# Another sequence for the same operations: a WKV recurrence and a mixer MLP on one core

## The chip, the core and the metric

The kernel runs on one NeuronCore of one Trainium2 chip. The metric is the device time of one execution in microseconds; the time before is the median of three runs, 478.63 us (478.45 to 481.3). Five engines work in parallel, each through its own queue in order: TensorE (PE, with its weight loads as PEld), VectorE (DVE), ScalarE (ACT), GpSimd (POOL) and SyncE (SP), which here only starts transfers. They wait for each other through semaphores.

## The reference

```python
def _attn_ref(r, k, v, w, u):            # (B,H,S,D) = (4, 8, 768, 48)
    for t in range(S):
        cur = einsum('bhd,bhe->bhde', u[None] * kt, vt)
        y[:, :, t] = einsum('bhd,bhde->bhe', rt, state + cur)
        state = wt[:, :, :, None] * state + einsum('bhd,bhe->bhde', kt, vt)

def _moe_ref(x, w_tok1, w_tok2, w_ch1, w_ch2):   # x: (4, 768, 384); d_tok 256, d_ch 1536
    h = maximum(xt @ w_tok1, 0) @ w_tok2         # xt: x with tokens and channels swapped
    u = x + h.transpose(0, 2, 1)
    return u + maximum(u @ w_ch1, 0) @ w_ch2
```

The output of the first function, its heads put side by side, is the `x` of the second.

## The kernel before

**Units.** A batch's 768 tokens fall into three units of 256, so four batches give twelve units, numbered 0 to 11. The recurrence runs in chunks of 64 tokens, four to a unit. Within a unit, for all eight heads at once:

- `load_part` and `load_w`, `load_v` bring k, r (tiles `rk`, for unit 2 a part of the tile `first`), the decays w and the values v. SP starts all of these.
- DVE scans the decays backwards (`ends`, L431 to L436) and forwards (`begins`, L443) and multiplies keys (L440) and queries (L446) by them.
- ACT multiplies keys by u (`own_u`, L331, tile `near`); PE makes the chunk's own products (`own_gram`) and the products with earlier tokens (`gram`), both at L315; DVE takes them into the tile `at` (`own_put` L458, `mask` L327).
- PE turns the keys (`tokens`, L345), ACT copies them out (`copied`, L350), PE makes the chunks' outer products in the PSUM tile `kv` (`carry`, L365).
- The state passes from chunk to chunk: ACT scales it into the tile `before` (`scaled`, L501, four instructions, called by0 to by3 below, one for each chunk) and PE adds it into `kv` by a product with the identity (`update`, L508, called up0 to up3; from unit 3 on DVE adds, L516). by1 needs up0, up1 needs by1, and so on into the next unit.
- PE multiplies queries with states (`across`, L380, called `before` in the sequence), ACT reads one column (`seen`, L389 or L392), PE adds the products within the chunks (`within`, L401, called `after`) and ACT puts the sum into `x` (`taken`, L407).
- ACT checks the decays' range (`ranges`, called small and large, L427).

**Weights** arrive as 64-bit words and are made into float32 in pieces of 1024 columns, three for the token mixer (t0 to t2) and nine for the channel mixer (c0 to c8). Each piece is a load (L261), two steps on ACT (plus L264, minus L267) and four on DVE (lead L270, two L273, value L277, sum L281).

**Mixers.** For batch 0, `hidden` (L947, called h0 to h11), its ReLU (`rectified`, L950), `back` (L958, with the sum into x at L960), `turn` (L969, copied to `xT` at L971), `up` (L993, ReLU L996) and `down` (L1004) run on float32 weights. For batches 1 to 3 `exact_mixing` runs the same in three float32r passes each (L667, L726, L741, L772 to L792), with weight parts that ACT, DVE and POOL split off ("forms", L579 to L601), some of which go to DRAM and come back through a ring of ten slots (L626).

**What sets the sequence.** Nothing is left to a scheduler. `strict(...)` ties each instruction to the one before it on its engine, in the order of its arguments. Before batch 0's second mixing half, these arguments are a list written out in the code (three units, three token pieces, the first channel piece). After that `interleaved(ORDER, ...)` merges ten streams of pieces; each digit of the string `ORDER` says which stream gives the next piece. `behind(gate, f)` adds a wait to a transfer: it isn't started before `gate` has run.

The first channel product (`up` at L993) is the point from which PE works through batch 0's channel mixer and everything that follows.

## Time and profile before

| | |
|---|---|
| three runs | 478.63 us median, 478.45 to 481.3 |
| the profiled execution, its own time | 478.31 us |
| its span, first to last instruction | 476.5 us |
| busy time on DVE, ACT, POOL | 344.6, 265.8, 54.2 us |
| bytes moved | 85.34 MB, mean 179 GB/s |

The span is what the trace shows; 1.8 us of the execution lie around it. A row of the timeline has the start in us from the span's start, the length in us, engine, line, operation, output and inputs, the count of instructions that follow each other, and in brackets the idle time of the engine before the row and what ended it. A PE row's length includes the drain of its last product, so that the start of the next row is the better end. A row of waits has engine, its line, what it waited for, us in total, how often, and the longest. A float32 product shows as two matmul records, so that the twelve h steps are 24 records.

### The profile page before, as it was taken

What the parts mean: (1) busy time and instruction counts of PE and PEld (TensorE: products, weight loads), DVE (VectorE), ACT (ScalarE), POOL (GpSimd) and SP (SyncE); (2) the same over time, 40 slices, a digit from 0 to 9 for tenths busy, and PEclk for the clock granted to TensorE, in tenths of its full rate; (3) what the DMA queues carried; (4) which work ended last, traced back from release to release, by engine and by line L of the source; (5) the groups of instructions that cost most, each with busy time, mean ns of one, the idle gap of its engine ahead of it and who ended that gap; (6) DMA issues with size and microseconds to landing.
All of it is one profiled execution on the core that took longest, in us unless ns stands there. A gap on an engine that the chain in (4) does not pass through costs nothing.

```text
span 476.5 us, 12778 instructions
## 1 busy us (share of the span) xinstructions
PE 459.1 (96%) x5322; PEld 409.6 (86%) x5322; DVE 344.6 (72%) x495; ACT 265.8 (56%) x606; POOL 54.2 (11%) x58
## 2 busy tenths in 40 slices
PE   3899999999999999999999999999999999999996
PEld 2776588856797668999999999999999999999995
DVE  7998797679598877876897998685587885235341
ACT  6699876674678856453747385351837554134140
POOL 1000000000000001231302002130304003032130
PEclk9999999999999999999999999999999999999999
DMA  8865745573584556963888842754784513336331
GB/s 313 317 221 217 188 169 191 180 275 99 152 228 138 177 179 207 284 186 100 252 283 232 294 154 56 198 173 141 215 227 150 167 61 84 115 101 199 86 99 54
DMA packets 45055, 85.34 MB, mean 179 GB/s; under 512 B 4736, under 2 KB 37376, under 8 KB 44992
## 3 DMA queue, kind: packets, MB, share of 16 engines
q1 hardware_dynamic: 44704, 84.37, 56.3%
q8 instruction: 43, 0.70, 0.6%
q14 instruction: 20, 0.16, 0.1%
q10 hardware_dynamic: 288, 0.10, 0.1%
HBM read 72.65 MB, written 11.80 MB: 177 GB/s over the span
## 4 chain that ended last, share of the span: by engine, by line
PE 90%; ACT 4%; DVE 2%; DMA 2%; issue 1%; SPq 0%; DVEq 0%; ACTq 0%
PE bank L1004 10%; PE bank L772 8%; PE bank L779 8%; PE bank L774 8%; PE bank L790 8%; PE bank L792 8%; PE bank L791 8%; PE bank L993 7%; PE bank L667 3%; PE bank L989 3%; PE bank L726 3%; PE bank L315 2%; PE bank L401 2%; PE bank L380 2%; PE kv_ps L365 2%; PE bank L669 2%
## 5 line engine op out<-in xcount | busy, mean ns | idle before, releaser
L765 POOL TENSOR_TENSOR z_high<-z_high 128x384 fp32r<-128x384 f32 x48 | 52.9, 1107 | 406.7 <-DMA ring<-third 186.8
L754 ACT ACTIVATE z_high<-bank 128x384 fp32r<-128x384 f32 x48 | 23.5, 489 | 58.1 <-PE bank L779 57.7
L772 PE MATMUL bank<-x_forms,forms 128*128 128x384 f32 x216 | 50.3, 341 | 0.0
L779 PE MATMUL bank<-z_more,forms 128*128 128x384 f32 x216 | 50.1, 340 | 0.0
L774 PE MATMUL bank<-x_forms,ring 128*128 128x384 f32 x216 | 49.3, 337 | 0.0
L761 DVE SCALAR_TENSOR_TENSOR z_high<-bank,z_high 128x384 fp32r<-128x384 f32 x48 | 26.5, 554 | 31.4 <-ACT z_high L754 29.4
L1004 PE MATMUL bank<-wch,z 128*128 128x384 f32 x144 | 48.1, 488 | 0.0
L790 PE MATMUL bank<-forms,z_high 128*128 128x384 f32 x140 | 47.8, 342 | 0.0
L792 PE MATMUL bank<-forms,z_high 128*128 128x384 f32 x140 | 47.1, 337 | 0.0
L791 PE MATMUL bank<-ring,z_high 128*128 128x384 f32 x140 | 47.1, 337 | 0.0
L798 DVE SCALAR_TENSOR_TENSOR x<-bank,x 128x384 f32<-128x384 f32 x35 | 18.8, 553 | 39.0 <-PE bank L792 38.9
L1004 PEld LDWEIGHTS bank<-wch,z 128*128 128x128 f32 x144 | 26.8, 190 | 17.2
L501 ACT ACTIVATE before<-state,to_end 112x48 f32<-112x48 f32 x132 | 33.1, 324 | 13.0 <-DVE state L516 7.6
L779 PEld LDWEIGHTS bank<-z_more,forms 128*128 128x128 f32 x216 | 39.0, 188 | 0.1
L772 PEld LDWEIGHTS bank<-x_forms,forms 128*128 128x128 f32 x216 | 38.3, 188 | 0.5
L774 PEld LDWEIGHTS bank<-x_forms,ring 128*128 128x128 f32 x216 | 38.6, 188 | 0.0
L993 PE MATMUL bank<-xT,wch 128*128 128x256 f32 x144 | 32.0, 381 | 0.0
L993 PEld LDWEIGHTS bank<-xT,wch 128*128 128x128 f32 x144 | 27.0, 190 | 3.7
L757 ACT ACTIVATE z_high<-z_high 128x384 fp32r<-128x384 f32 x48 | 25.2, 525 | 3.5
L790 PEld LDWEIGHTS bank<-forms,z_high 128*128 128x128 f32 x140 | 26.3, 188 | 0.2
L791 PEld LDWEIGHTS bank<-ring,z_high 128*128 128x128 f32 x140 | 26.3, 188 | 0.0
L792 PEld LDWEIGHTS bank<-forms,z_high 128*128 128x128 f32 x140 | 26.3, 188 | 0.0
(243 smaller groups left out, 961.2 us busy)
## 6 DMA issues: line engine op xcount, KB each, us to landing
ring<-third SPq DMA_DIRECT2D x144, 192.0 KB, 3.4
raw<-in_words_ch_dram SPq DMA_DIRECT2D x8, 1023.8 KB, 4.8
rk<-in_rk_dram SPq DMA_DIRECT2D x36, 192.0 KB, 5.2
near<-in_near_dram SPq DMA_DIRECT2D x8, 768.0 KB, 5.0
w<-in_w_dram SPq DMA_DIRECT2D x10, 520.5 KB, 5.1
vt<-in_v_dram SPq DMA_DIRECT2D x12, 384.0 KB, 5.0
out_dram<-x SPq DMA_DIRECT2D x17, 192.0 KB, 2.8
third<-forms SPq DMA_DIRECT2D x12, 192.0 KB, 3.3
```

Source lines behind the costliest of these rows:

```text
L501: act.mul(t[:ROWS, a], state[bt, g][:ROWS, a], by_last(c, j)[:, a:a + 1])
L757: act.mul(z_form(jt, 2), z_form(jt, 0).bitcast(f32), 1.0 / BASE)
L761: dve.scalar_tensor_tensor(z_form(jt, 1), a, 0.0, z_form(jt, 0).bitcast(f32), op0=ALU.max, op1=ALU.subtract)
L765: pool.tensor_add(z_form(jt, 2), z_form(jt, 2).bitcast(f32), z_form(jt, 1).bitcast(f32))
L772: pe.matmul(a, up[m], xf(0)[:, m], start=m == 0, stop=False)
L774: pe.matmul(a, low[:, m], xf(1)[:, m], start=False, stop=False)
L779: pe.matmul(banks["a", jt], joint, xf(2)[:, m], start=False, stop=m == 2)
L790: pe.matmul(a, z[0], up, start=first, stop=False, skip_group_check=True)
L791: pe.matmul(a, z[1], held[bt, s, half, 1, jt], start=False, stop=False, skip_group_check=True)
L792: pe.matmul(a, z[2], joint, start=False, stop=last, skip_group_check=True)
L993: pe.matmul(ps, now["wch1"][:, jt // 4, m, ts(jt % 4, 128)], xT[:, m, ts(s, SEG)], start=(m == 0), stop=(m == DM // 128 - 1))
L1004: pe.matmul(ps, zs[s][:, jt, ts(n, 128)], now["wch2"][:, jt, :], start=(jt == 0), stop=(jt == NJ - 1))
```

## The change

The list of arguments is replaced by a string `FIRST` of names, which a small loop hands to `strict` one by one (`name<gate` stands for `behind`), and `ORDER` gets another sequence of the same digits in the same numbers. Apart from `ranges`, which now goes by the two names small and large, no operation, tile, pool or buffer changes. The lines of the kernel move by 11 (L508 before is L519 after).

```diff
+FIRST = (
+    "masks k0 0.ends 0.begins 0.own0 0.own1 r0 0.own2 0.own3 0.own 0.small 0.keys 0.queries k1 1.own0 1.own1 1.own2 w1 1.ends 0.put v0 "
...
+    "1.tokens 1.begins 1.copied0 1.put 0.up3 0.gram 1.by0 1.copied1 0.before k2<1.ends 2.own0 1.queries t0.plus 2.own1 v1<0.by2 1.carry "
...
+    "c0.load<1.gram t1.two 2.up2 2.gram 2.mask h3 2.by3 t2.plus 2.before h4 2.seen t2.minus t1.value t1.sum t2.lead 2.after 2.taken1 "
+    "2.taken0 t2.two 2.taken2 h5 h6 c2.load<1.tokens t2.value h7 c0.plus t2.sum h8 c0.minus c0.lead c0.two h9 h11 h10 relu1 relu0 back0 "
+    "c0.value c1.load<2.own 1.large 1.small rk3 w3<2.by3 2.large v3"
+)
 ORDER = (
-    "888008088078808800000888484440800840804080880804808844804088488400448088408008888080080884808884040488844488888084840880880"
...
+    "400488880088880088080044088000088880400878888048888880000008004884444888888088880000484444408880044088880888844448000408"
...
-    strict(lambda: load_part(0, 1), masks, e0["ends"], e0["own_u"][0], e0["own_u"][1], e0["own_u"][2], e0["own_u"][3], e0["begins"],
...
+    for name in FIRST.split():
+        name, _, gate = name.partition("<")
+        strict(behind(named[gate], named[name]) if gate else named[name])
```

Rows of the engines' order follow: line, operation, output and inputs, shape, and a count. `rk_88` holds r and k of unit 0 (later of unit 3), `rk_89` those of unit 1, `first` those of unit 2.

PE before, from unit 1's first update on (the four rows of L508 are its updates up0 to up3): the updates stand between single products.

```order
L508 MATMUL kv_ps<-before,ident 112x192
L315 MATMUL gram<-first,near 64x64 x32
L508 MATMUL kv_ps<-before,ident 112x192
L345 MATMUL k_ps<-ident,first 128x112 x8
L508 MATMUL kv_ps<-before,ident 112x192
L315 MATMUL gram<-rk_89 64x64 x32
L508 MATMUL kv_ps<-before,ident 112x192
L380 MATMUL y_ps<-before,rk_89 64x48 x32
```

PE after, from the same update on.

```order
L519 MATMUL kv_ps<-before,ident 112x192
L412 MATMUL y_ps<-vt,at_92 64x48 x32
L519 MATMUL kv_ps<-before,ident 112x192 x2
L326 MATMUL gram<-rk_89 64x64 x32
L356 MATMUL k_ps<-ident,first 128x112 x8
L391 MATMUL y_ps<-before,rk_89 64x48 x32
L326 MATMUL gram<-first,near 64x64 x32
L519 MATMUL kv_ps<-before,ident 112x192
```

Unit 1's second and third update now follow each other, and its fourth stands behind its own gram, unit 2's transposes, unit 1's product with the states and unit 2's own products.

ACT before, from unit 0's large-range check on: `first` in the third row is unit 2's k, and `first` as the second input of L501 holds unit 0's decays.

```order
L427 ACTIVATE junk,flags<-first,most 112x1041
L501 ACTIVATE before<-kv_ps,first 112x48 x8
L331 ACTIVATE near<-first,u_col 112x2x128 x2
L501 ACTIVATE before<-kv_ps,first 112x48 x4
L331 ACTIVATE near<-first,u_col 112x2x128
L350 COPY kT<-k_ps 128x384
L264 ACTIVATE raw<-raw,rebias 128x1024
L389 COPY seen<-y_ps 128x2
L331 ACTIVATE near<-first,u_col 112x2x128
L350 COPY kT<-k_ps 128x384
L501 ACTIVATE before<-kv_ps,to_end_93 112x48 x4
```

ACT after, from unit 0's large-range check on.

```order
L438 ACTIVATE junk,flags<-first,most 112x1041
L512 ACTIVATE before<-kv_ps,first 112x48 x4
L342 ACTIVATE near<-rk_89,u_col 112x2x128
L512 ACTIVATE before<-kv_ps,first 112x48 x8
L278 ACTIVATE raw<-raw,rebias 128x1024
L361 COPY kT<-k_ps 128x384
L512 ACTIVATE before<-kv_ps,to_end_93 112x48 x4
L361 COPY kT<-k_ps 128x384
L342 ACTIVATE near<-first,u_col 112x2x128
L275 ACTIVATE raw<-raw,rebias 128x1024
L342 ACTIVATE near<-first,u_col 112x2x128
L400 COPY seen<-y_ps 128x2
```

Unit 0's by3 no longer stands behind the two instructions that read unit 2's k, and unit 1's by0 now comes ahead of them; unit 0's `seen` moves behind both steps of t0.

ACT before, at the end of the first stretch, from the last of three range checks on: c1's plus and minus (L264, L267), two copies to `xT`, c2's plus and minus, two more copies, and then `near<-rk_88`, which reads unit 3's k.

```order
L427 ACTIVATE junk,flags<-to_end_93,most 112x1041
L264 ACTIVATE raw<-raw,rebias 128x1024
L267 ACTIVATE raw<-raw,rebias 128x1024
L971 COPY xT<-bank_875 128x3x128
L971 COPY xT<-bank_877 128x3x128
L264 ACTIVATE raw<-raw,rebias 128x1024
L267 ACTIVATE raw<-raw,rebias 128x1024
L971 COPY xT<-bank_873 128x3x128
L971 COPY xT<-bank_875 128x3x128
L331 ACTIVATE near<-rk_88,u_col 112x2x128 x4
```

ACT after, from the last of the three range checks on.

```order
L438 ACTIVATE junk,flags<-first,most 112x1041
L342 ACTIVATE near<-rk_88,u_col 112x2x128 x2
L275 ACTIVATE raw<-raw,rebias 128x1024
L278 ACTIVATE raw<-raw,rebias 128x1024
L982 COPY xT<-bank_875 128x3x128
L982 COPY xT<-bank_877 128x3x128
```

Two of the four instructions that read unit 3's k now stand ahead of c1's steps.

Further on, unit 3's product with the states (L380), which stood behind 84 matmul records of `down` on PE, stands behind the first 40.

## The prediction

> **What bounds the kernel now.** I read the page first, then PE's waits in the stretches 0 to 62 us and from 62 us on, then the timelines of PE, ACT and DVE over the first 62 us. The page:

> ```profile
> span 476.5 us, 12778 instructions
> PE 459.1 (96%) x5322; PEld 409.6 (86%) x5322; DVE 344.6 (72%) x495; ACT 265.8 (56%) x606; POOL 54.2 (11%) x58
> PE 90%; ACT 4%; DVE 2%; DMA 2%; issue 1%; SPq 0%; DVEq 0%; ACTq 0%
> ```

> PE is busy 459.1 of 476.5 us and carries 90% of the chain of waits. PE's waits, for the two stretches apart (total, times, longest):

> ```profile
> PE gram L315 <- DMA rk<-in_rk_dram: 7.6, 1, 7.6
> ...
> PE bank L401 <- ACT seen L392: 0.6, 2, 0.3
> PE bank L401 <- issue: 0.5, 1, 0.5
> ```

> The first row is the wait for the first data. From 62 us on PE waits 1.1 us in all. The number of PE's instructions stays the same, so the later 414 us can win 1.1 us at most and lose without limit; the rest must come from the first 60 us. PE's timeline there, from the chunks' first outer products to the first `up`:

> ```profile
> 13.70 1.50 PE L365 MATMUL kv_ps<-vt,kT 64*48 64x48 f32 x64
> 17.11 1.99 PE L315 MATMUL gram<-rk,near 48*64 48x64 f32 x64
> 19.02 0.98 PE L508 MATMUL kv_ps<-before,ident 112*112 112x192 f32 x2
> ...
> 28.89 0.93 PE L345 MATMUL k_ps<-ident,first 112*128 112x112 f32 x8
> ...
> 30.53 1.16 PE L315 MATMUL gram<-rk 48*64 48x64 f32 x64
> ...
> 32.13 1.15 PE L380 MATMUL y_ps<-before,rk 48*64 48x48 f32 x64
> ...
> 39.78 0.91 PE L947 MATMUL h_ps<-x,wtok 128*128 128x384 f32 x2
> ...
> 42.55 1.15 PE L401 MATMUL y_ps<-vt,at 64*64 64x48 f32 x64
> 43.62 1.24 PE L947 MATMUL h_ps<-x,wtok 128*128 128x384 f32 x3
> 45.38 3.81 PE L947 MATMUL h_ps<-x,wtok 128*128 128x384 f32 x11 [0.53 <-issue]
> 49.04 1.66 PE L958 MATMUL kv_ps<-h,wtok 128*128 128x384 f32 x4
> ...
> 59.08 3.19 PE L993 MATMUL bank<-xT,wch 128*128 128x256 f32 x14
> ```

> From 28.89 on PE has little idle time; before, it has much. What it waits for there is the state's way through units 0, 1 and 2: ACT scales (L501), PE adds (L508), in turn. ACT's rows on that way, and two that stand in it:

> ```profile
> 12.04 0.48 ACT L350 COPY kT<-k_ps 128x384 f32<-128x384 f32 x1 [0.27 <-PE k_ps L345]
> ...
> 15.27 0.87 ACT L501 ACTIVATE before<-kv_ps,first 112x48 f32<-112x48 f32 x4 [0.80 <-PE kv_ps L365]
> ...
> 20.33 0.91 ACT L331 ACTIVATE near<-first,u_col 112x256 f32<-112x256 f32 x2 [2.24 <-DMA first<-in_rk_dram]
> 21.14 0.85 ACT L501 ACTIVATE before<-kv_ps,first 112x48 f32<-112x48 f32 x4
> ...
> 24.57 0.94 ACT L501 ACTIVATE before<-kv_ps,to_end 112x48 f32<-112x48 f32 x4
> ...
> 30.64 0.87 ACT L501 ACTIVATE before<-kv_ps,to_end 112x48 f32<-112x48 f32 x4 [0.30 <-PE kv_ps L508]
> ...
> 32.24 0.87 ACT L501 ACTIVATE before<-kv_ps,first 112x48 f32<-112x48 f32 x4 [0.36 <-PE kv_ps L508]
> ...
> 35.36 0.87 ACT L501 ACTIVATE before<-kv_ps,first 112x48 f32<-112x48 f32 x4
> ```

> At 20.33 ACT has stood 2.24 us for unit 2's k, with unit 0's by3 (21.14) behind it, though the update that by3 reads had ended at 19.02 + 0.98 = 20.00.

> **The change part by part.** All operations stay, so each step is a difference of starting times. Rows overlap by about 0.1 us: an ACT operation starts 0.75 to 0.8 us after the start of four L501 (0.87), 0.4 after a copy (0.48) or a `near` (two in 20.33 to 21.14), and I take 1.15 for a plus or minus (1.20 at 53.35, below). An update on PE with its signals takes 0.7: 32.24 less 30.64 and 0.87.

> *Step 1, unit 0.* gram0 moves behind unit 1's transposes, so the outer products no longer wait for it (13.70) but for ACT's copies. These are done at 12.04 + 0.48 = 12.5, and as they change places, the one that is read first comes last: about 12.9. by1 so starts at 14.5 instead of 15.27. From by1 to the end of the update that by3 reads it was 20.00 - 15.27 = 4.7 us, with own1 between two updates, where it still is: by3 can start at 19.3, and with unit 2's k out of its way it does, 1.8 us earlier than 21.14.

> *Step 2, unit 1.* Behind by3 ACT now has minus, copy, by0, copy, `near`, plus, `near`, `seen`. By0 starts at 19.3 + 0.8 + 1.15 + 0.4 = 21.65 (before 24.57), but `seen` only at 24.8, since both steps of t0 stand ahead of it; `after` of unit 0 and by1 follow at 25.0. With two `near` and a copy to x (1.25 us) ahead of by2, that starts at 25.0 + 0.75 + 1.25 = 27.0, up2 on PE at 27.9, by3 at 28.55: 2.1 us ahead of 30.64. PE, done with `after` and up1 at 26.55, stands 1.35 us for by2.

> *Step 3, the lead is spent.* up3 now stands behind gram1, unit 2's transposes, unit 1's product with the states and unit 2's own products. By the rows 30.53, 28.89 and 32.13, less some 0.1 us of drain, these take 1.1 + 0.9 + 1.05 + 1.1 = 4.15 us: PE, which leaves up2 at 28.3, reaches up3 at 32.45, and unit 2's by0 starts 0.65 later at 33.1, 0.85 us after 32.24. PE itself has then done what it began at 32.13 and took 1.05 for in before, and is 0.3 us ahead once up3 is counted.

> *Step 4, unit 2.* ACT has both steps of t1 between by0 and by1: by1 at 33.1 + 0.75 + 2.3 = 36.15 (before 35.36). PE leaves up3 at 32.85, works through `after`, outer products, up0 and three h steps (1.1; 0.9, the 1.50 at 13.70 made shorter as gram is from 1.99 to 1.16; 0.4; six records as at 45.38, 1.95) and up1 until 37.6, and stands until by2 is done at 38.7: 1.1 us. Then up2, gram, h, states, h (0.4 + 1.1 + 0.85 + 1.1 + 0.85 us, a lone h step as at 39.78 less its drain) bring `after` of unit 2 to 43.0. Before: 42.55.

> *Step 5, to the back products.* 14 records of h follow, in before 3 from 43.62 and 11 from 45.38. Three records at 0.33 us end at 44.6, so 0.8 us of this is a pause, whose row names "issue" and no releaser. Without it the h steps, 4.65 us, end at 43.0 + 1.05 + 4.65 = 48.7, with it at 49.5; I take it as gone, as nothing in the order makes it. Against 49.04 this wins 0.35. But the last h step now feeds the ReLU that the first back product reads:

> ```profile
> 49.24 0.49 ACT L950 ACTIVATE h<-h_ps 128x384 f32<-128x384 f32 x1 [0.80 <-PE h_ps L947]
> 53.35 1.20 ACT L264 ACTIVATE raw<-raw,rebias 128x1024 int16<-128x1024 int16 x1
> ...
> 59.27 0.48 ACT L971 COPY xT<-bank 128x384 f32<-128x384 f32 x1 [0.25 <-PE bank L969]
> 59.65 1.70 ACT L331 ACTIVATE near<-rk,u_col 112x256 f32<-112x256 f32 x4
> ```

> A ReLU starts 0.2 us after its h step and takes 0.49, so back starts at 48.7 + 0.75 = 49.45, 0.4 us after 49.04.

> *Step 6, to `up`.* ACT's ReLUs end at 49.4 (before 49.24 + 0.49 = 49.73), and the three range checks follow at once. Then two of the four `near` of unit 3 (half of 1.70 us) stand ahead of c1's plus: 53.35 - 0.3 + 0.85 = 53.9. DVE's lead of c1 waits for ACT in before:

> ```profile
> 55.70 0.69 DVE L270 TENSOR_TENSOR raw<-raw 128x1024 int16<-128x1024 int16 x1 [1.83 <-ACT raw L267]
> ```

> It moves to 56.25, and the sum that `up` needs and the last copy to `xT` (59.27) move by the same 0.55. **First term: `up` runs 0.5 us later**; 1.3 if the pause returns, and 1.95 earlier if PE's two waits in steps 2 and 4 (1.35 and 1.1 us) don't come.

> *Step 7, after 62 us.* The 0.6 us for `seen` are two places where `after` follows directly on the unit's product with the states. In unit 8 ten us of other products now stand between: -0.3. The wait with "issue" stays. Of waits that don't exist yet the trace has no price: at the near end nothing, at the far end the rival of unit 3 below (2 us). I take nothing, as the longest in before is 0.5 us. **Second term: -0.3.**

> The sum is +0.2 on the profiled execution's 478.31 us (span 476.5 and 1.8 around it): **forecast 478.5 us**, with an own range of 477.3 to 479.8. The median of the runs is 0.3 above that execution, which is within what this sum can tell.

> **The rivals.**

> *PE's two waits don't come (faster).* ACT's operations could start closer than my spacings. Then PE gains 2.45: 476.05. For it: by0 of unit 1 comes 2.9 us earlier. Against: each spacing is measured in the same stretch. 0.17.

> *The array's clock opens earlier.* Here the row of the stretch 12 to 24 us (PE's busy time, the granted clock and DMA share at the end):

> ```profile
> 12.00:24.00 12.00, 10.60 (x255) 9.11 (x254) 10.84 (x9) 7.84 (x24) 0.00 (x0) 1.00 0.87 314
> ```

> The granted clock reads 1.00, yet the 64 products that take 1.16 us at 30.53 took 1.99 at 17.11 and the update 0.98 at 19.02. In the new order PE has no pause from 16.4 on; if it ran fast by 16.4, the updates up1 and up2 would each take 0.4 us less, and by3 and all behind it would come 0.8 earlier: 477.8. [...] 0.06.

> *Unit 3 waits for the forms (slower).* Its product with the states stood behind 84 records of `down`, now behind 40:

> ```profile
> 94.24 15.64 PE L1004 MATMUL bank<-wch,z 128*128 128x384 f32 x48
> ...
> 122.86 0.96 PE L380 MATMUL bank<-before,rk 48*64 48x48 f32 x42
> ```

> At 15.48/48 = 0.32 us a record PE asks for it at 94.24 + 12.9 = 107.1 instead of 122.86. Its by2 and by3 now stand on ACT between the forms' first steps (L579), and these wait for c8's sum, whose room they take:

> ```profile
> 100.83 1.23 DVE L281 TENSOR_TENSOR wch<-wch,raw 128x1024 f32<-128x1024 f32 x1
> 102.15 3.78 ACT L579 ACTIVATE forms<-wch 128x768 fp32r<-128x768 f32 x5 [1.44 <-DVE wch L281]
> 105.84 1.00 ACT L501 ACTIVATE before<-state,to_end 112x48 f32<-112x48 f32 x4
> ```

> From 102.15 on: two L579 (3.78/5 = 0.76 each), by2 (1.0, as at 105.84), two L579, by3: 107.2, just when PE asks. From there on each us by which c8 is late is a us of PE. DVE's idle time ahead of a piece's lead reaches 1.83 us at 55.70; as late as that, it costs 1.9: 480.5. Against: c4's and c6's values move ahead of unit 3's work on DVE, and c8's load hangs on c6's. It decides when c8's sum ends after 102. 0.14.

> *Unit 3's k stops ACT (slower).* `near` in step 6 wants it at 53.05. In before:

> ```profile
> 41.76 11.99 SPq L188 DMA_DIRECT2D rk<-in_rk_dram  x8
> rk<-in_rk_dram SPq DMA_DIRECT2D x8, 192.0 KB, 11.9
> xT<-in_words_tok_dram SPq DMA_DIRECT2D x1, 1023.8 KB, 4.8
> ```

> At 11.9 us to landing, and issued behind c1's load, which waits for t1's value on DVE (unit 2's gram ends at 40.2, then two operations of 1.2 us like the one at 100.83), it would be issued at 43 and land at 55 and hold ACT, and c1 and `xT` behind it, for 2 us: 480.6. Against: before, c1 and c2 were issued just ahead; now c2 goes some 10 us earlier, w and v go behind, and one word load alone lands in 4.8 us, so that k should be there by 50. 0.08.

> *The forecast* has 0.52. The remaining 0.03 is for several at once.

> **How the numbers follow.** A measurement of this kernel can tell about 1% from no change, 4.8 us. No case reaches that alone: faster by over 1% takes the first rival, the clock's 0.8, the 0.8 us of waits after 62 us that I left, and as much again, 0.05; slower by over 1% takes both slow rivals and a third wait of their size, 0.07; within 1% 0.88. The range goes down to the first rival with the clock's or those waits' part (476.05 less 1.2, half way to having both): 474.9; and up to a slow rival with the pause and its own doubt of 0.5: 481.8.

> **What would show it.** Right: by3 of unit 0 near 19.3, unit 1's by0 near 21.7, unit 2's by0 near 33, first `up` within 0.6 us of 59.6, PE's waits after 62 us under 1.5 us in all. Wrong: an `up` before 57.5 or after 61, a PE wait at unit 3's states near 107, an ACT wait for `rk` near 53, or a new releaser among PE's waits with over 2 us.

## The result and the profile after

| | before | after |
|---|---|---|
| time, median (lowest to highest) | 478.54 us (477.09 to 481.3), 4 runs | 500.9 us (499.06 to 502.19), 4 runs |
| ratio, 95% interval | | 1.046 (1.040 to 1.052) |
| the profiled execution's span | 476.5 us | 500.5 us |
| last h step starts | 48.7 us | 61.9 us |
| first `up` | 59.1 us | 72.2 us |
| from there to the first product that reads `z_high` as a form | 135.7 us | 143.1 us |
| from there to the end | 281.7 us | 285.3 us |

The change makes the kernel 22 us slower; the forecast was no change. In the profiled executions the difference is 24 us: 13.1 of it are there at the first `up`, 7.4 come up to about 215 us, 3.6 behind that.

The page of after:

```profile
span 500.5 us, 12770 instructions
...
PE 472.3 (94%) x5322; PEld 418.9 (84%) x5322; DVE 346.5 (69%) x495; ACT 267.8 (54%) x606; POOL 59.3 (12%) x58
...
PEclk9975999999999999999999999999999899999998
...
PE 92%; ACT 3%; issue 3%; DMA 1%; DVE 0%; SPq 0%; DVEq 0%; ACTq 0%
```

The same 5322 matmul records keep PE busy 13 us longer, and the row of the granted clock has slices at 7 and 5. That row of before:

```profile
PEclk9999999999999999999999999999999999999999
```

"Issue" has gone from 1% to 3% of the chain of waits. PE's waits, first from 0 to 62 us, then from 62 us on:

```profile
PE gram L326 <- ACT near L342: 8.7, 1, 8.7
PE kv_ps L376 <- issue: 3.8, 2, 1.9
PE kv_ps L519 <- ACT before L512: 3.4, 3, 1.4
```

```profile
PE bank L783 <- DVE z_high L772: 2.9, 1, 2.9
PE bank L326 <- issue: 2.5, 2, 1.7
```

Lines of after stand 11 below those of before (L508 is now L519). PE's timeline of after, at the places that the steps of the prediction speak of:

```profile
21.74 1.88 PE L326 MATMUL gram<-rk 48*64 48x64 f32 x64
...
26.71 1.08 PE L376 MATMUL kv_ps<-vt,kT 64*48 64x48 f32 x41 [1.90 <-issue]
...
30.40 0.58 PE L519 MATMUL kv_ps<-before,ident 112*112 112x192 f32 x2
32.38 0.58 PE L519 MATMUL kv_ps<-before,ident 112*112 112x192 f32 x2 [1.41 <-ACT before L512]
32.89 1.43 PE L326 MATMUL gram<-rk 48*64 48x64 f32 x64
...
35.93 1.96 PE L391 MATMUL y_ps<-before,rk 48*64 48x48 f32 x64
37.67 2.23 PE L326 MATMUL gram<-first,near 48*64 48x64 f32 x64
39.83 0.98 PE L519 MATMUL kv_ps<-before,ident 112*112 112x192 f32 x2
...
44.78 1.44 PE L376 MATMUL kv_ps<-vt,kT 64*48 64x48 f32 x44 [1.93 <-issue]
...
46.92 3.97 PE L958 MATMUL h_ps<-x,wtok 128*128 128x384 f32 x6
...
62.98 1.56 PE L969 MATMUL kv_ps<-h,wtok 128*128 128x384 f32 x4 [0.58 <-ACT h L961]
...
72.15 1.03 PE L1004 MATMUL bank<-xT,wch 128*128 128x256 f32 x4
```

Twice PE stops for 1.9 us in the middle of outer products whose operands are all there. And from 33 to 50 us everything is slow: 64 matmul records with the states take 1.96 us (1.15 in before), six records of h steps 3.97 (11 took 3.81). The windows table of after, cut along the steps of the clock, which are 3.41 us apart (columns: stretch; length; busy time and instructions on PE, PEld, DVE, ACT, POOL; granted clock; DMA share; GB/s):

```profile
23.38:26.79 3.41, 1.51 (x91) 1.38 (x87) 3.01 (x3) 1.85 (x4) 0.00 (x0) 1.00 0.66 263
26.79:30.21 3.42, 3.42 (x103) 2.87 (x107) 1.47 (x3) 1.27 (x5) 0.00 (x0) 0.50 0.02 6
30.21:33.62 3.41, 2.00 (x68) 1.40 (x65) 1.56 (x2) 2.75 (x11) 0.00 (x0) 1.00 0.57 197
33.62:37.03 3.41, 3.41 (x80) 3.01 (x73) 2.42 (x2) 2.84 (x7) 0.00 (x0) 0.50 0.83 317
37.03:40.44 3.41, 3.41 (x99) 3.02 (x94) 0.50 (x1) 0.16 (x1) 0.00 (x0) 0.50 0.85 281
...
47.27:50.68 3.41, 3.41 (x6) 1.66 (x5) 0.00 (x0) 1.24 (x5) 0.00 (x0) 0.50 0.00 0
50.68:54.10 3.42, 2.46 (x70) 1.77 (x69) 0.18 (x1) 2.81 (x11) 0.00 (x0) 1.00 0.00 0
```

The stretch with the first pause (PE busy 1.51) runs at 1.00 and the next one at 0.50; the stretch with the wait for ACT at 32.38 (busy 2.00) again at 1.00, and then come five at 0.50, to 50.68. In before the clock stays at 1.00 from 22.6 us to the end. The records of the clock begin with its first rise, at 23.38 us in after and 22.60 in before. For the time ahead of that the views print 1.00 and all nines, but the products were slow there: 64 records took 1.99 us at 17.11 in before and 1.16 at 30.53. So that time is counted as half clock below.

The later losses: near 204 us ACT stops 4.8 us, PE behind it. Three answers of after: ACT's timeline, the waits for the tile `third`, and SP's queue:

```profile
209.30 0.49 ACT L765 ACTIVATE z_high<-bank 128x384 fp32r<-128x384 f32 x1 [4.82 <-issue]
```

```profile
ACT z_high L765: 4.8, 1
```

```profile
201.26 3.17 SPq L637 DMA_DIRECT2D ring<-third  x7
204.53 0.38 SPq L605 DMA_DIRECT2D third<-wch  x1
```

`z_high` takes the room that the last store of a third of the weights reads, and that store is now queued behind seven ring loads; in before it was issued at 180.57 us, ahead of them:

```profile
180.57 0.37 SPq L594 DMA_DIRECT2D third<-wch  x1
183.52 3.17 SPq L626 DMA_DIRECT2D ring<-third  x7
```

The rest are pauses of PE put to issue, 1.05 us at 163 and 1.88 at 388 us (from start to start of a product), and a stretch at half clock behind the stops at 207 and 388.

### The profile page after: what moved, and what is told of

The parts are those of the page before. It is cut to its first block, busy times and chain, and to the rows that moved or that the text cites. A ratio compares the mean times of both kernels' runs of the same rounds, so it can differ in the third digit from the quotient of the medians.

```text
span 500.5 us, 12770 instructions
## 1 busy us (share of the span) xinstructions
PE 472.3 (94%) x5322; PEld 418.9 (84%) x5322; DVE 346.5 (69%) x495; ACT 267.8 (54%) x606; POOL 59.3 (12%) x58
## 4 chain that ended last, share of the span: by engine, by line
PE 92%; ACT 3%; issue 3%; DMA 1%; DVE 0%; SPq 0%; DVEq 0%; ACTq 0%
PE bank L1015 10%; PE bank L801 8%; PE bank L783 8%; PE bank L803 7%; PE bank L785 7%; PE bank L802 7%; PE bank L790 7%; PE bank L1004 6%; PE bank L678 3%; PE bank L737 3%; PE bank L1000 3%; PE kv_ps L376 2%; PE bank L326 2%; PE h_ps L958 2%; PE gram L326 2%
## 5 line engine op out<-in xcount | busy, mean ns | idle before, releaser
L776 POOL TENSOR_TENSOR z_high<-z_high 128x384 fp32r<-128x384 f32 x48 | 58.0, 1220 | 425.5 <-DVE z_high L772 422.0
L783 PE MATMUL bank<-x_forms,forms 128*128 128x384 f32 x216 | 50.8, 343 | 2.9 <-DVE z_high L772 2.9
L790 PE MATMUL bank<-z_more,forms 128*128 128x384 f32 x216 | 50.3, 341 | 0.0
L1015 PE MATMUL bank<-wch,z 128*128 128x384 f32 x144 | 49.2, 491 | 0.0
L801 PE MATMUL bank<-forms,z_high 128*128 128x384 f32 x140 | 48.8, 349 | 0.0
L803 PE MATMUL bank<-forms,z_high 128*128 128x384 f32 x140 | 47.7, 341 | 0.0
L783 PEld LDWEIGHTS bank<-x_forms,forms 128*128 128x128 f32 x216 | 38.7, 190 | 3.8 <-DVE z_high L772 3.2
L1015 PEld LDWEIGHTS bank<-wch,z 128*128 128x128 f32 x144 | 26.5, 190 | 16.4
L1004 PE MATMUL bank<-xT,wch 128*128 128x256 f32 x144 | 32.0, 381 | 0.3 <-ACT xT L982 0.3
L1004 PEld LDWEIGHTS bank<-xT,wch 128*128 128x128 f32 x144 | 27.0, 190 | 4.4 <-ACT xT L982 0.7
L801 PEld LDWEIGHTS bank<-forms,z_high 128*128 128x128 f32 x140 | 26.7, 191 | 0.5
L802 PEld LDWEIGHTS bank<-ring,z_high 128*128 128x128 f32 x140 | 26.7, 190 | 0.0
L803 PEld LDWEIGHTS bank<-forms,z_high 128*128 128x128 f32 x140 | 26.6, 190 | 0.0
## 6 DMA issues: line engine op xcount, KB each, us to landing
ring<-third SPq DMA_DIRECT2D x144, 192.0 KB, 3.3
raw<-in_words_ch_dram SPq DMA_DIRECT2D x8, 1023.8 KB, 5.2
rk<-in_rk_dram SPq DMA_DIRECT2D x36, 192.0 KB, 5.8
out_dram<-x SPq DMA_DIRECT2D x17, 192.0 KB, 2.8
third<-forms SPq DMA_DIRECT2D x12, 192.0 KB, 4.6
```

Of the source, the lines that this page charges most:

```text
L776: pool.tensor_add(z_form(jt, 2), z_form(jt, 2).bitcast(f32), z_form(jt, 1).bitcast(f32))
L783: pe.matmul(a, up[m], xf(0)[:, m], start=m == 0, stop=False)
L790: pe.matmul(banks["a", jt], joint, xf(2)[:, m], start=False, stop=m == 2)
L801: pe.matmul(a, z[0], up, start=first, stop=False, skip_group_check=True)
L802: pe.matmul(a, z[1], held[bt, s, half, 1, jt], start=False, stop=False, skip_group_check=True)
L803: pe.matmul(a, z[2], joint, start=False, stop=last, skip_group_check=True)
```

## What stops PE

By this estimate a block must come while PE works through the one before. Between 21.9 and 24.1 us, and then between 24.1 and 26.7 us, the DMA engines of after moved (queue, packets, MB, share):

```profile
q1 hardware_dynamic: 114, 0.90, 97.7%
```

```profile
q1 hardware_dynamic: 162, 0.58, 56.1%
q8 instruction: 1, 0.02, 2.3%
```

PE entered the block at 21.91 and the transfer of its successor began at 24.16, after 2.2 us in which the DMA engines were full of data. Worked out from the packets and PE's records:

```
                     block entered   transfer starts   PE stops   PE resumes   DMA share, 4 us before
after, to 705            21.91           24.16           24.61       26.71           0.99
after, to 1473           38.04           42.56           42.57       44.78           0.86
after, to 4033          161.47          162.16          163.36      164.41           0.11
after, to 9153          385.76          387.90          388.51      390.39           0.66
before, to 705           17.60           20.33             -           -             0.88
before, to 1985          40.70           43.03           44.37       45.38           0.52
before, to 6593         251.70          253.47          255.50      256.17           0.93
```

Over all kernels of this study PE stopped over 0.5 us at such a place 50 times; in 49 of them it resumed 2.2 to 2.8 us after the start of the transfer (2.2 to 2.7 in the six of the table). So PE pauses when it uses up a block in less time than the next one takes to start and to arrive. Full DMA engines are one reason. Put each transfer to the block that it supplies: where the DMA share was under 0.1 (168 transfers), it began at most 1.7 us after PE had entered the block before (1.14 us behind 164.41 of after); where the share was over 0.8 (348 transfers), up to 8.2 us after (8.18 behind 58.05 of after). But full engines are not needed. PE entered one block of small products at 161.47 us and had used it up in 1.89 us. The next transfer started after 0.69 us, with the DMA engines idle, and PE still stopped for 1.05 us. Eleven of the 50 stops are of this kind, with a share under 0.1 and up to 1.75 us long.

In before the outer products and gram products were spread between waits; the change put unit 0's gram products, state products and unit 1's outer products in a row, 176 matmul records from 21.74 us.

## The experiments

Theory A: late blocks of PE's stream, the half clock that follows, and the late store are the loss. The rival: the new sequence is slow in itself, by the waits between ACT and PE, and the clock only shows it. In the table "half" is the time at half clock between 20 and 60 us. Each kernel has two to seven runs, and its ratio is against runs of before next to them (medians 477.9 to 479.6 us). The last three columns come from one execution of each kernel.

| kernel | time, us | ratio (95%) | last h step | first `up` | half, us |
|---|---|---|---|---|---|
| before | 478.5 | 1 | 48.7 | 59.1 | 2.6 |
| the change | 500.9 | 1.046 (1.040 to 1.052) | 61.9 | 72.2 | 23.9 |
| old_head | 496.0 | 1.038 (1.023 to 1.053) | 48.9 | 59.5 | 8.2 |
| new_head | 490.2 | 1.025 (1.014 to 1.037) | 61.3 | 71.8 | 26.6 |
| store_first | 492.6 | 1.031 (1.020 to 1.042) | 58.3 | 68.5 | 19.4 |
| shift | 500.5 | 1.047 (1.036 to 1.058) | 57.1 | 67.3 | 17.0 |
| shift16 | 494.6 | 1.034 (1.029 to 1.039) | 56.2 | 66.4 | 16.2 |
| gram_back | 498.1 | 1.041 (1.038 to 1.044) | 57.5 | 67.7 | 20.5 |
| before_shift | 492.7 | 1.030 (1.024 to 1.035) | 57.3 | 67.7 | 13.7 |
| fill | 498.6 | 1.042 (1.026 to 1.058) | 61.0 | 71.2 | 9.0 |
| loads_later | 494.6 | 1.036 (1.029 to 1.042) | 56.8 | 67.0 | 14.9 |
| loads_store | 490.1 | 1.026 (1.020 to 1.033) | 55.7 | 65.9 | 11.0 |
| before_traffic | 480.4 | 1.004 (1.000 to 1.008) | 50.3 | 60.7 | 6.8 |
| all | 490.4 | 1.025 (1.022 to 1.027) | 54.2 | 64.5 | 3.9 |
| all_seen | 492.4 | 1.029 (1.025 to 1.033) | 50.8 | 64.9 | 1.0 |
| no_fill | 493.4 | 1.030 (1.025 to 1.034) | 55.0 | 68.6 | 15.3 |
| all_even | 489.0 | 1.019 (1.014 to 1.024) | 51.6 | 63.0 | 1.2 |

### The two parts of the change alone

```diff
 old_head:  FIRST = before's sequence of the head, as names;  ORDER = the change's digits
 new_head:  FIRST = the change's names;  ORDER = before's digits
```

> The head sequence of before with the order string of the change. Theory A (the loss of 22 us has two separate parts: about 13 us in the head, which the head sequence alone makes, and about 11 us in the body, which the order string alone makes, at 163, 204 to 214 and 388 to 395 us): h steps end near 49 us as before, first `up` near 59 to 60 us, and the whole takes 485 to 491 us. Rival B (the body's losses only follow from the head being late, since transfers and pauses meet elsewhere): within 1.5 us of before, 477 to 480 us.

> The head sequence of the change with the order string of before. Theory A: h steps end near 63 us, TensorE pauses of about 2 us near 24 and 42 us, granted clock at half for most of 26 to 50 us, and the whole takes 489 to 494 us (before + 11 to 15). Rival B (the order string matters only as far as the head shifts it): 498 to 503 us, as the change.

Both parts cost by themselves. new_head loses 12 us, all in the head (71.8 at the first `up`, then as before, 135.7 us to `z_high`). old_head loses 18, more than theory A had expected (485 to 491 us), with a head like before's: 146.3 us from the first `up` to `z_high` instead of 135.7, with pauses of 1.75 us at 151 and 2.64 at 379 and 3.1 us of PE behind the late store, each with a stretch at half clock behind it. That is more than the 11 us which the body loses in the change itself. The sequence sets where a pause can come, but its length differs between executions: the same block came 1.75 us late at 151 us in old_head and 1.05 us late at 163 us in the change, both times with the DMA engines idle (busy under 10% from 148 to 160 us in old_head, 0.00 from 161.47 to 162.16 us in the change). A head scatters too: the same one gives a first `up` at 68.5, 71.8 and 72.2 us in store_first, new_head and the change.

### The late store

```diff
 ORDER, digits 355 to 357 (counted from 0)
-008
+800
```

> The change, with the last store of a third of the weights put ahead of the seven ring loads that stand before it in SyncE's queue. Theory C (ScalarE's 4.8 us at 204 to 209 us is a wait for that store to land, since its z tile takes the room that the store reads; TensorE's 2.9 us and the half clock from 211 us follow): that wait falls under 1 us, the clock stays at 1.0 from 204 to 216 us, and the whole takes 4 to 6 us less, 494 to 497 us. Rival D (the transfers are as late in either order, the DMA engines being full, so that the ring loads are waited for instead): 499 to 502 us, with TensorE waiting near 207 us for a ring load.

ACT's wait for the store is gone, the clock stays at 1.00 there, and first `up` to `z_high` takes 138.8 us instead of 143.1: theory C, 4.3 us. The time fell by 8.3 us, more than expected, the profiled span by 10.9, and the rest is not the store's: the head, which is the same, was 3.7 us faster in this execution, with a second pause of 1.00 us instead of 1.93, and the stretch behind `z_high` 3.0, with a shorter pause near 380 us and no half clock behind it.

### Shifting the blocks

Unused products ahead of everything, while PE waits for its first load, shift the blocks against the work: 32 of them in shift, 16 in shift16, and 56 in before_shift, which otherwise is before. One such product is four instructions of PE's queue, two weight loads and two matmul records, so the shifts are by 128, 64 and 224 instructions (10870 and 10806 records instead of 10742, 10980 instead of 10756). The expectations below counted two for each, and so worked with half the shift.

```diff
+    def spin():
+        t = ps_m.tile([128, 512], f32, name="spin", tag="m")
+        for _ in range(32):
+            pe.matmul(t[:T, :T], ident[:D, :T], ident[:D, :T], start=True, stop=True)
-masks k0 0.ends
+spin masks k0 0.ends
```

> The change, with 32 products (64 instructions of TensorE's queue) that nothing uses put ahead of everything, while TensorE waits for its first load; it shifts the 256-instruction blocks of TensorE's stream by 64 against the work. Theory A1 (the pauses put down to issue stand where a block of the stream is fetched too late: their places are instruction 193 of a block in all five cases seen; the half clock follows from the pauses): the pauses at 24.3 and 42.6 us are gone or under 1 us, the clock stays up for most of 24 to 50 us, h steps end at 50 to 56 us, and the whole takes 487 to 495 us. Rival A2 (the sequence itself is slow, its waits between ScalarE and TensorE set the head, and the clock is only a witness): the pauses may move, but h steps end at 61 to 64 us and the whole takes 499 to 503 us.

> The change, with 16 unused products (32 instructions) ahead of everything; 32 instructions moved the pauses but made another one, since the block ended at 25.8 us while the DMA engines were full. Worked out from the times at which the change reaches each instruction, a shift of 32 gives every block of the head at least 3.8 us from the start of the one before it to its own, where the change gave 2.7. Theory A1: both pauses under 1 us, the clock keeps 1.0 until the wait for ScalarE near 29 us at least, h steps end at 52 to 58 us, the whole takes 489 to 497 us. Rival A2: h steps end at 61 to 64 us, 499 to 503 us.

> Before, unchanged but for 56 unused products (112 instructions) ahead of everything, while TensorE waits for its first load. The block of the stream that ends after instruction 1360 of before is then used up in 2.5 us, and is asked for near 31 us, when the DMA engines are full. Theory A1: a pause of 1 to 2.5 us put down to issue near 33 to 34 us; if it is over 1.3 us, the clock falls to half one window later, and the whole takes 484 to 495 us; if it is shorter, 479 to 482 us. Rival A2 (the places of the blocks don't matter): no such pause, 477 to 480 us.

In shift the two pauses at 24.6 and 42.6 us are gone, and a new one of 2.28 us stands at 26.0, in other products (L412) but again at a block's edge (instruction 961). The expected time was wrong, as I counted pauses that go and none that come, and with the wrong shift. shift16 came out inside theory A's range, with 1.51 us left at that edge, but as its places too were worked out with half the shift, that is partly luck. before_shift, before's own sequence with 56 products ahead, loses 14 us. PE's timeline and two rows of its windows table:

```profile
1.53 12.10 PE L1118 MATMUL spin<-ident 48*64 48x64 f32 x111 [1.53 <-POOL ident masks.py:199]
...
23.97 0.96 PE L356 MATMUL k_ps<-ident,rk 112*128 112x112 f32 x8 [1.34 <-issue]
...
31.07 0.98 PE L412 MATMUL y_ps<-vt,at 64*64 64x48 f32 x26 [0.70 <-issue]
...
165.48 0.46 PE L326 MATMUL bank<-rk 48*64 48x64 f32 x16 [3.28 <-issue]
```

```profile
23.78:27.19 3.41, 2.26 (x54) 1.96 (x56) 2.55 (x5) 1.78 (x7) 0.00 (x0) 1.00 0.99 369
27.19:30.60 3.41, 2.59 (x51) 1.81 (x45) 3.38 (x3) 3.36 (x10) 0.00 (x0) 0.50 0.35 142
```

The place I named (33 us) was wrong, and the 56 products were not free. They run until 13.5 us, and the first product that is used starts at 13.32 us instead of 7.59, some 1.5 us of this because its data came later. So 5.7 of the 8.6 us by which the first `up` is late are no late blocks. With the unused products ahead the clock also rose already at 16.95 us (22.60 in before); PE then stood more for ACT and ahead of `k_ps` (23.97, no edge of a block; DVE finished the keys that it reads at 23.87), and the clock fell at 27.19 for 13.7 us. In the head, then, this run says little on the blocks.

The body is clearer. From the first `up` to `z_high` it takes 142.6 us instead of 135.7, and the 6.9 us are two late blocks, of 1.62 us at 134 and 3.50 at 162 us from start to start, and a stretch at half clock behind the second, by estimate 1.7 us. There before owes its time to where its blocks happen to end as well as to its sequence.

### Breaking the row of small products

```diff
-0.tokens 0.copied1
+0.tokens 0.gram 0.copied1
...
-0.up3 0.gram 1.by0
+0.up3 1.by0
```

> The change, with one entry of the head's list moved: unit 0's 64 gram products go back to their place of before, right after unit 0's key transposes, so that they no longer stand directly ahead of the 48 state products and the 64 outer products. Theory A1 (TensorE's stream of instructions runs dry where a block of 256 is used up in less time than its successor takes to arrive, and the clock falls after the pause): no pause over 1 us near 24 us, no fall of the clock at 26 us, h steps end at 50 to 57 us, the whole takes 488 to 496 us. Rival A2 (the sequence of waits sets the head, whatever the clock does): the pause goes, but h steps end at 60 to 64 us and the whole takes 498 to 503 us.

The pause near 24 us goes, as expected, but the outer products of unit 0 come later with the products ahead of them, a smaller pause (0.45 us by the timeline) comes at the next edge, PE waits 1.28 us for DVE at 20.0 and 1.41 for ACT at 26.8, and the clock is at half for 20.5 us, nearly as long as in the change (23.9). Against theory A as I had put it: without the long pause the head was still 8.6 us late.

### Holding the clock up

Ten products that nothing reads go where PE waits for ACT, ahead of unit 1's third state product.

```diff
+    def fill():
+        t = ps_m.tile([128, 512], f32, name="fill", tag="m")
+        for _ in range(10):
+            pe.matmul(t[:, :128], ident, ident, start=True, stop=True)
-1.by2 0.taken0 t0.two 1.up2
+1.by2 0.taken0 t0.two fill 1.up2
```

> The change, with ten 128x128 products that nothing uses put ahead of unit 1's third state product, where TensorE waits 1.4 us for ScalarE (30.98 to 32.38 us). Theory A3 (that wait, 1.4 us of a window of 3.41, is what takes the clock to half from 33.62 to 50.68 us, and the half clock costs the head more than the pauses themselves): the clock stays at 1.0 after 33.6 us until the second pause at least, h steps end 3 to 8 us earlier than 61.9, at 54 to 59 us, and the whole takes 492 to 498 us. Rival A4 (the pauses alone set the clock, the wait doesn't count): clock as in the change, 499 to 503 us.

The clock does stay at 1.00, to 42.69 us, and the head wins nothing: PE, faster now, runs its stream dry three times. Its timeline:

```profile
27.11 0.69 PE L376 MATMUL kv_ps<-vt,kT 64*48 64x48 f32 x41 [2.93 <-issue]
...
37.02 0.38 PE L391 MATMUL y_ps<-before,rk 48*64 48x48 f32 x10 [1.61 <-issue]
...
43.58 0.57 PE L412 MATMUL y_ps<-vt,first 64*64 64x48 f32 x12 [3.79 <-issue]
```

8.3 us of pauses, where the change has 3.8, take the place of the half clock. The clock is thus not the cause by itself: a faster PE waits longer for its blocks. The run changes more than the clock, though. The first of the three pauses stands ahead of the filling products, and these shift the blocks behind them by 40 instructions.

### Moving the loads

```diff
-2.own3 t1.load 2.keys
+2.own3 2.keys
...
-r2<0.tokens 0.taken2
+r2<0.tokens t1.load<1.by1 0.taken2
...
-c0.load<1.gram t1.two
+c0.load<2.by1 t1.two
...
-h6 c2.load<1.tokens
+h6 c2.load<2.by1
```

> The change, with three loads of 1 MB put later in SyncE's queue and held until TensorE's run of small products is over: the second load of the token weights behind unit 1's second scaling (it was queued at 18.7 us and moved data until 25.5), the first two of the channel weights behind unit 2's second scaling (34.4 and 36.8 us, data until 42.5). No instruction of TensorE, VectorE or ScalarE moves. Theory A5 (a block of TensorE's stream comes late because its transfer stands behind data in full DMA engines, so what the sequence costs is where loads and dense products meet): the pauses near 24 and 42 us fall under 1.2 us each, the clock is at half for less than 10 us of 24 to 55, h steps end at 50 to 56 us, and the whole takes 486 to 494 us. Rival A6 (the products use up a block faster than it can come, whatever the DMA engines do): pauses of 1.5 us or more stay at the same instructions, h steps end at 59 to 63 us, the whole takes 497 to 503 us.

> The same later loads, and the last store of a third of the weights ahead of the seven ring loads as well. If both act and are independent: the loads' result less 4 to 6 us, so 480 to 489 us under theory A5, with only the short pauses near 160 and 385 us left; under rival A6, 491 to 497 us.

> Before, with four loads of 0.52 MB that nothing reads (into a weight tile that is written whole later), held until unit 2's second scaling, near 36.3 us, where the DMA engines of before stand idle until 41 us. The block that ends after instruction 1728 is asked for near 37 us and needed at 40.7. Theory A5: its transfer starts 1.5 to 4 us later than the 37.5 us of before, TensorE pauses 1 to 3.5 us near 40.7 us, and if that is over 1.3 us the clock falls at the next window: 481 to 492 us. Rival A6 (the DMA load doesn't matter): no pause there, 477 to 480 us.

loads_store has the store of store_first besides; before_traffic is before with four loads that nothing reads. No instruction of PE, DVE or ACT moved in loads_later, and the last h step starts 5.1 us earlier: the pause at 42.6 us is gone, the first is 1.42 us. Theory A5 holds for the second pause. For the head as a whole the support is weaker, as the unchanged head of store_first had its last h step at 58.3 us; the times of the runs (494.0 and 495.2 us, against 499.1 to 502.2 in the change) do not overlap. What stays is the wait for ACT (1.57 us at 27.9) with 13.7 us of half clock behind it, and a pause of 0.98 us where the moved loads now run. loads_store adds 4.5 us for the store, as expected; both came out at or just over the upper ends. before_traffic did little: as data waits in its head had moved, the extra loads met another block, the pause of 1.01 us at 44.4 became 1.47 at 45.5, and the clock stayed at 1.00 behind it. The direction is right, but the difference of the times (480.4 to 479.1 us) is not clear of noise and says nothing against the rival.

### Everything together

```diff
 spin (16), fill (10), the store ahead of the ring loads, and
 all:       t1.load<1.by1   t2.load<2.by1   c0.load<2.by1    c2.load<2.by1
 all_seen:  t1.load<1.by1   t2.load<2.by1   c0.load<2.seen   c2.load<2.seen
 no_fill:   as all_seen, without fill
 all_even:  t1.load<1.by1   t2.load<2.by0   c0.load<2.by1    c2.load<2.seen
```

> The change with everything that the runs before pointed to: 16 unused products (32 instructions) ahead of the stream, so that no block of the head ends inside a run of small products; the second and third loads of the token weights and the first two of the channel weights held until unit 1's and unit 2's second scalings; ten unused 128x128 products ahead of unit 1's third state product, where TensorE waits 1.4 to 1.6 us for ScalarE; and the last store of a third of the weights ahead of the ring loads. Theory A (late blocks of the stream, the half clock that follows on them and on that wait, and the store are the whole loss; the sequence of the change as such costs what was forecast, about nothing): no pause over 1 us before 60 us, clock at 1.0 from about 22 us on, h steps end at 49 to 53 us, first `up` at 60 to 64 us, the whole 478 to 486 us. Rival A2 (there is a further loss in the sequence of the head that none of these touches): h steps end at 55 us or later, the whole takes 488 us or more.

> The last kernel (all), with the first two loads of the channel weights held further, until unit 2's `seen` copy near 44 us, so that no load runs from about 41 to 44 us, when the block that ended at 45 us is asked for. Theory A (late blocks and the clock are the rest): no pause over 1 us in 20 to 56 us, clock 1.0 from about 21 us on, h steps end at 49.5 to 51.5 us (54.2 in the last kernel), first `up` at 60 to 62 us, the whole 484 to 488 us with the pause at 377 us still there, 480 to 484 us if that one stays away. Rival A2 (the sequence of the head costs something itself): h steps end at 53 us or later, the whole 489 to 492 us.

> The kernel above without the ten filling products, so that TensorE stands 1.4 to 1.6 us for ScalarE ahead of unit 1's third state product. Theory A3 (a window of 3.41 us with about 1.3 us or more of standing takes the next one to half, and it stays there for 10 us or more because products at half clock are slow to fill one): the clock falls near 31 us for 7 to 17 us, h steps end 2.5 to 6 us later than above. Rival A4 (only pauses of the stream take the clock down): clock 1.0 throughout, h steps end within 1 us of the above.

> The kernel with all mends, with the third load of the token weights held until unit 2's first scaling (about 35 us), the first of the channel weights until its second (about 39 us), the second of the channel weights until its `seen` copy (about 44.5 us). Theory A (nothing is lost in the sequence itself): no pause over 1.3 us before 65 us, h steps end at 50 to 52 us, first `up` at 60 to 62 us, clock 1.0 from 21 us until the pause near 380 us at least; the whole 479 to 486 us, the upper half with that pause. Rival A2 (the sequence loses some us wherever the loads stand): first `up` at 63 us or later, 488 to 492 us.

In all the clock held from 20.5 us until a pause of 2.36 us at 45, just where the moved loads filled the DMA engines (70 to 80% busy from 36.5 to 48.7 us). all_seen takes them away and the last h step starts at 50.8, as theory A said; but now ACT waits for those loads (1.74 us at 49.84) and for unit 3's k, which the same queue brings behind them (3.51 us at 60.13). PE stands behind these waits (1.66 us at 51.3, 2.6 at 62), and what was won is lost again ahead of `up`. no_fill shows what ACT's wait costs through the clock. Its PE timeline and windows, and then those of all_seen at the same place:

```profile
28.55 0.98 PE L519 MATMUL kv_ps<-before,ident 112*112 112x192 f32 x2 [1.37 <-ACT before L512]
```

```profile
25.03:28.45 3.42, 1.75 (x66) 1.26 (x58) 3.02 (x4) 2.71 (x12) 0.00 (x0) 1.00 0.49 134
28.45:31.86 3.41, 3.31 (x69) 2.73 (x70) 1.08 (x3) 2.67 (x8) 0.00 (x0) 0.50 0.74 290
```

```profile
27.03 2.40 PE L1125 MATMUL fill<-ident 128*128 128x128 f32 x20
29.27 0.49 PE L519 MATMUL kv_ps<-before,ident 112*112 112x192 f32 x2
```

```profile
24.42:27.84 3.42, 2.86 (x76) 2.44 (x76) 3.02 (x4) 3.10 (x12) 0.00 (x0) 1.00 0.25 43
27.84:31.25 3.41, 3.41 (x86) 3.10 (x85) 1.70 (x3) 2.46 (x11) 0.00 (x0) 1.00 0.93 366
```

The clock falls at 28.45 for 13.7 us, and the last h step starts 4.2 us later, within theory A3's range. Of this little is left at the end: the whole takes 1.0 us more than all_seen, which has a late block of 2.2 us at 381 that no_fill is spared. The 1.3 us of standing in theory A3, which other expectations use too, was the author's estimate, and fill goes against it as a border: the stretches from 22.20 to 29.03 us, with PE busy 1.98 of 3.42 and 1.93 of 3.41 us, had the clock at 1.00 behind them.

all_even has the lowest time of the mended kernels, 489.0 us, and the clock stays at 1.00 from 21.2 us on, but it misses both forecasts: the first `up` at 63.0 is between them, the time in the rival's range. Its span is 11.3 us over before's. 2.9 are there at the last h step (pauses of 0.3 to 1.05 us at four edges, 2.2 us together, and the first data 0.8 us later), 1.0 more at the first `up` (ACT stands 1.82 us for unit 3's k, PE 0.94 behind it), 2.3 up to `z_high`, 5.1 behind it. PE's waits from 62 us on:

```profile
PE bank L801 <- issue: 3.3, 1, 3.3
PE bank L412 <- ACT seen L403: 1.8, 2, 1.6
PE bank L1004 <- ACT xT L982: 1.1, 1, 1.1
PE bank L980 <- DVE x L971: 0.9, 1, 0.9
```

That is 7.1 us in these rows, where before has 1.1 in all, and 3.3 of it is another late block, at 378 us. No kernel of this study beats before.

## Why the prediction was wrong

**Step 1** held: by1 of unit 0 at 14.9 (forecast 14.5), by3 at 19.7 (19.3), unit 1's by0 at 21.9 (21.65), though the first product started 1.1 us later. That 1.1 us is no effect of the change: the same head has its first product at 7.77 to 8.72 us in the other executions, and before's own head at 8.89 in before_traffic.

**Step 2** is the first that failed. It let PE be "done with `after` and up1 at 26.55", with every product at the length of its row. PE stopped 1.90 us in the outer products, ran at half clock from 26.79 to 30.21 and was done at 31.0. The wait for by2 then came almost as forecast, 1.41 us for 1.35, but that is luck: it came 4.4 us late, and by2 started 2.7 us after by1, not 2.0, as ACT in turn waited for PE's `after`. I priced the stand itself and not what it does to the clock.

**Steps 3 and 4** took 4.15 us for four groups of products from rows at full clock; at half clock they took 6.94 (32.89 to 39.83). `after` of unit 2 came at 56.5, not 43.0. Added up along the path: 1.1 us for the first data, 3.8 for the two pauses, and by estimate about 7 for products at half clock (2.8 in step 3, 1.9 in six records of h steps, the rest in the other groups): 11.9 of the 13.1 us at `up`.

**Step 5** took the pause of 0.8 us ahead of the h steps "as gone, as nothing in the order makes it". It is the sentence that hid the mechanism: that pause of before stands at instruction 1985, a block's edge, and the order has its part in where such a pause falls. The row said "issue", and I did not ask what issue was. The ReLU that now feeds the back product cost 0.58 us of PE, forecast 0.4: right.

**Step 6** was right in kind: two `near` stand ahead of c1's plus, and PE waits 0.32 us for `xT` at 73.5.

**Step 7** took new waits "as nothing" for want of a row. The late store (4.3 us) could have been found: the order shows a store passing behind seven loads on SP, and `z_high` takes its room. I followed the queue for loads only. The pauses at 163 and 388 us are blocks again.

**The rivals.** Those that I priced as slower, unit 3's forms and unit 3's k, did not come in the change; unit 3's k came when the channel loads were held back (3.51 us of ACT in all_seen). The clock was among the rivals, but on the side of gain alone: I let a stretch without pauses open it earlier, for which no row of before spoke, and never asked what a stretch with pauses would close. The stretch without pauses did come, from 15.86 to 24.6 us, and the clock opened no earlier for it (23.38, 22.60 in before); no run shows the 0.8 us that this rival was to win. In after pauses of 1.90 and 1.41 us were enough: the stretches that they fall in (PE busy 1.51 and 2.00 of 3.41 us) have half clock behind them. The signs I had named as wrong did show: an `up` after 61, and new releasers over 2 us among PE's waits.

What the runs do not settle: whether the new sequence costs nothing once no block is late. all_even comes within 3 us of before at the last h step, and 2.2 of these are pauses, but its whole is 10 us slower, and the waits that my own shifts of loads made are in it. So for some 10 of the 22 us the rival, a loss in the sequence itself, is not excluded.

## What to carry to other kernels

A sequence that packs small products densely was limited here by how fast its instructions arrived (in after PE used up a block in 1.89 us from 161.47 us on and stopped for 1.05): count instructions per microsecond on the busiest engine, and look at each idle time put to issue, where it stands in blocks of the stream, before taking it for noise. Where many small operations run in a row, keep large loads out of that stretch (moving three of them won 6 us in loads_later), and price a stand of an engine with its clock: 1.4 us of standing cost 4 us of the head here (no_fill, though only 1 us of the whole). And when an order is searched with measured durations, durations measured in the old order are not those of the new one (1.15 us in before and 1.96 in after for the same 64 records with the states).

## What the runs showed of the hardware

The clock did not follow PE's busy time. In after a stretch of 3.41 us with PE busy throughout left the next at half (33.62 to 40.44 above), and one with 2.46 us kept it (50.68 to 54.10). In before_shift a stretch with 2.25 us kept it at 1.00 and the next one, with 2.26 us, left it at half:

```profile
20.36:23.78 3.42, 2.25 (x68) 1.63 (x68) 3.42 (x3) 0.87 (x4) 0.00 (x0) 1.00 0.94 349
```

What goes with it more closely in the head of after is the work done, by the author's estimate: for each matmul record its active rows times its active columns, over 128 x 128, times the columns streamed, summed over the records that start in a stretch. The clock in the stretch and in the next:

```
after       sum    clock   next          after       sum    clock   next
19.96      1504      -      1.0          37.03      1278     0.5     0.5
23.38       723     1.0     0.5          40.44       804     0.5     0.5
26.79      1347     0.5     1.0          43.86      1074     0.5     0.5
30.20      1212     1.0     0.5          47.27      1920     0.5     1.0
33.62      1336     0.5     0.5          50.68      1740     1.0     1.0
```

The clock stayed down for 17 us while, at half clock, the small products of 33.62 to 40.44 us, without any pause, made 1280 to 1340 in a stretch, and it rose behind the stretch with the h steps (1920). The sum does not settle the clock: in the two traces of before and after, half clock also stands behind 1536 and 1644 (after, from 207.70 and 388.60 us), and full clock behind 1255 (before, from 19.19 us). No run tested it by itself, and what sets the clock was not shown.
